# GroupNorm on one core: TensorE as a loop over the tiles, loads relayed into one count, and the last two tiles loaded in halves and stored in quarters

## The chip, the cores and the metric

The kernel runs on one core of one Trainium2 chip. The metric is the device time in microseconds (us) of that core. Most times below are medians of four or five runs, one of them profiled. The kernel before took 633.99 to 634.82 us, median 634.18, in the call that also timed the changed kernel.

## The reference

```python
# x: (128, 1024, 32, 16) bf16, g and b: (1024,) bf16, 32 groups of 32 channels
def reference(x, g, b):
    G = 32
    xr = x.reshape(B, G, C // G, H, W)
    mu = xr.mean(axis=(2, 3, 4), keepdims=True)
    var = ((xr - mu) ** 2).mean(axis=(2, 3, 4), keepdims=True)
    xn = ((xr - mu) / jnp.sqrt(var + 1e-5)).reshape(B, C, H, W)
    return xn * g[None, :, None, None] + b[None, :, None, None]
```

It reads 134.2 MB and writes as much. One tile is 4 samples times 32 groups on 128 partitions, with 16384 bf16 values (32 KB) in each: 4 MB. There are 32 tiles.

## The kernel before

SBUF holds a ring of six tile slots. SyncE issues all loads and stores. TensorE sums a tile with 32 matmuls against an identity matrix, VectorE turns the sum into the negative mean, ScalarE squares the tile around the mean in two passes of 7.12 us, and VectorE then scales and shifts in place, 32 operations a tile. Tile i+6 is loaded into the slot that tile i was stored from.

```python
SLOTS, RUN, MM_FREE = 6, 2, 512          # F = 16384 values a partition, NT = 32 tiles, NMM = 32

def on_sync(e):
    def load(j):
        if j >= SLOTS:
            e.wait_ge(st[j % SLOTS], 16 * (j // SLOTS))       # the slot's store has landed
        e.dma_start(out=slot(j), in_=x_v[j]).then_inc(ld[j % SLOTS], 16)
    for j in range(SLOTS):
        load(j)
    for i in range(NT):
        e.wait_ge(s_done, i + 1)
        e.dma_start(out=o_v[i], in_=slot(i)).then_inc(st[i % SLOTS] if i + SLOTS < NT else s_fin, 16)
        if i % RUN == RUN - 1:                                # two stores, then two loads
            first = i + 1 + SLOTS - RUN
            for j in range(first, min(first + RUN, NT)):
                load(j)
    e.wait_ge(s_fin, 16 * SLOTS)

def on_tensor(e):                                             # unrolled: 1024 matmuls in the program
    ...
    for i in range(NT):
        e.wait_ge(ld[i % SLOTS], 16 * (i // SLOTS + 1))
        if i >= 2:
            e.wait_ge(s_mean, i - 1)
        par = i % 2
        for k in range(NMM):
            last = e.matmul(out=ps[:, par * MM_FREE : (par + 1) * MM_FREE], lhsT=eye[:],
                            rhs=slot(i)[:, k * MM_FREE : (k + 1) * MM_FREE],
                            start=(k == 0), stop=(k == NMM - 1))
        last.then_inc(s_sum, 1)

def on_vector(e):                                             # a loop over the tiles, addresses from registers
    ...
    with nc.Fori(0, NT, 1, engines=[e.engine], head_slot={e.engine: 128}) as i:
        ...                                                   # mean, 1/std, scale, bias
        for k in range(KC):                                   # KC = 32
            a = ring[:, bass.ds((i % SLOTS) * F + k * HW, HW)]
            last = e.tensor_scalar(out=a, in0=a, scalar1=scl[:, k : k + 1], scalar2=bia[:, k : k + 1],
                                   op0=ALU.mult, op1=ALU.add)
        e.drain()
        e.sem_inc(s_done, 1)
```

## Time and profile before

| what | value |
| --- | --- |
| time | 634.18 us (633.99 to 634.82) |
| span of the profiled run | 632.4 us |
| DMA traffic | 268.4 MB, mean 425 GB/s |
| busy share | ACT 76%, DVE 60%, PE 42% |
| last data packet ends / last landing / span ends | 630.63 / 631.11 / 632.37 us |

These are lines of the profile's page of the kernel before: the span, the DMA and bandwidth rows of the span in 40 slices, the DMA queues with packets and MB, and the head of the chain that ended last.

```profile
span 632.4 us, 5262 instructions
...
DMA  8999999999999999999999999999999999999986
GB/s 365 430 430 421 435 431 430 431 431 431 431 426 431 433 435 433 432 435 427 433 431 426 435 433 429 430 427 433 433 433 434 435 435 435 431 430 431 431 386 276
...
q1 hardware_dynamic: 9216, 268.44, 98.8%
q8 instruction: 8, 0.13, 0.1%
...
DMA 69%; ACT 19%; PE 3%; DVE 2%; issue 2%; SPq 1%; DVEq 1%; ACTq 0%
```

The DMA row is at nine or more tenths from the second slice to the third last, and the bandwidth is level at about 431 GB/s. No engine is busy more than 76%. The sixteen DMA engines therefore bound the kernel. The bandwidth falls only in the last two slices, and that is what the change aims at. Queue 8 shows eight packets of instructions (16 KB each, 0.90 to 1.01 us): the unrolled TensorE program being fetched.

The chain of waits of the kernel before, its last part cut to the longest pieces (start, length, what), shows how it ends:

```profile
436.26 38.11 DMA out_dram<-ring
475.24 38.34 DMA out_dram<-ring
513.99 29.02 DMA out_dram<-ring
543.03 19.50 DMA ring<-in_x_dram
562.58 9.91 PE ps L135 x32
573.67 7.12 ACT ja L157
```

The chain runs through one store after the other and crosses to compute only at 562.6 us, for the last two tiles. A view of the last work on the engines of the kernel before (start, length, engine and line):

```profile
612.68 3.31 DVE L214 TENSOR_SCALAR ring<-ring,scl,bia  x10
616.05 0.33 SPq L103 DMA_DIRECT2D out_dram<-ring  x1
```

VectorE finishes at 615.99 us and the last store goes out at 616.05. This looks as if compute ended the kernel. The semaphore records say otherwise. Each transfer adds 16 to its semaphore, and the sixteen come apart. (That each is one DMA engine's is my reading: between 100 and 400 us 16.0 packets are under way on average, and a transfer is 128 packets of 32 KB, eight for each of sixteen.) The last store's first increment came at 626.96 us and its last at 631.11. The bandwidth rows of the DMA view from 600 to 640 us (40 slices of 1 us) of the kernel before show the hole that this leaves:

```profile
DMA  9999799999899663949999599930000000000000
GB/s 492 492 492 393 328 426 492 459 459 426 360 393 524 295 262 131 426 197 524 459 524 492 229 393 492 492 131 33 33 33 0 0 0 8 0 0 0 0 0 0
```

Between 613 and 616 us part of the engines have nothing to do (the row falls to six and three tenths), because the store isn't issued yet. From 627 us on only a few engines still move data, 33 GB/s, and from 628.6 us on one alone. That one had not been idle at all: it went from the store of tile 30 straight to that of tile 31.

### The profile page before, as it was taken

The page shows a single profiled execution, that of the slowest core. Times are in us where ns is not written, and L with a number is a line of the kernel's source. Part 1 is how long each engine was busy: PE and PEld are TensorE (multiplying, and loading weights), DVE is VectorE, ACT ScalarE, POOL GpSimd, SP SyncE. Part 2 cuts the span into 40 slices and gives each one's busy share as a digit, 9 for nine tenths or more (in the row PEclk, how much of TensorE's full clock was granted, in tenths as well). Part 3 has the DMA queues.
Part 4 walks back from the last instruction along what each step waited for, and adds up shares of the span by engine and source line. Part 5 has one row for each costly group of instructions (what it writes and reads, how often), then busy time and mean ns, then how long its engine had stood idle before and what let it go on. Part 6 is the DMA issues. An engine that isn't in the chain of part 4 may idle for free.

```text
span 632.4 us, 5262 instructions
## 1 busy us (share of the span) xinstructions
PE 265.1 (42%) x1025; PEld 107.4 (17%) x1025; DVE 378.0 (60%) x1189; ACT 481.1 (76%) x194; POOL 0.8 (0%) x6
## 2 busy tenths in 40 slices
PE   1987609064180641806327063270723608146000
PEld 0332203021030210302103021130301203012000
DVE  0047777777757277572765727567375672747770
ACT  0499999999979499593995949769597694967920
POOL 0000000000000000000000000000000000000000
PEclk9978759668595675956759577595875958759555
DMA  8999999999999999999999999999999999999986
GB/s 365 430 430 421 435 431 430 431 431 431 431 426 431 433 435 433 432 435 427 433 431 426 435 433 429 430 427 433 433 433 434 435 435 435 431 430 431 431 386 276
DMA packets 9321, 268.58 MB, mean 425 GB/s; under 512 B 1120, under 2 KB 1120, under 8 KB 1120
## 3 DMA queue, kind: packets, MB, share of 16 engines
q1 hardware_dynamic: 9216, 268.44, 98.8%
q8 instruction: 8, 0.13, 0.1%
q10 hardware_dynamic: 96, 0.00, 0.0%
q14 instruction: 1, 0.01, 0.0%
HBM read 134.22 MB, written 134.22 MB: 425 GB/s over the span
## 4 chain that ended last, share of the span: by engine, by line
DMA 69%; ACT 19%; PE 3%; DVE 2%; issue 2%; SPq 1%; DVEq 1%; ACTq 0%
DMA out_dram<-ring 64%; ACT ja L157 18%; DMA ring<-in_x_dram 5%; PE ps L135 3%; DVE ring L214 2%; DVEq L218 1%; SPq L103 1%; SPq L97 1%; ACT var L167 0%; DVEq L214 0%; ACTq L166 0%; ACTq L157 0%; ACT rstd L171 0%; DVE jd L185 0%; DVEq L200 0%
## 5 line engine op out<-in xcount | busy, mean ns | idle before, releaser
L157 ACT ACTIVATE ja<-ring,nm 128x8192 fp8e5 x64 | 455.8, 7122 | 116.8 <-DVE jd L185 111.4
L135 PE MATMUL ps<-ring,eye 128*128 128x512 bf16 x1024 | 264.9, 425 | 303.2 <-DMA ring<-in_x_dram 297.2
L214 DVE TENSOR_SCALAR ring<-ring,scl,bia x1024 | 333.6, 406 | 7.5 <-issue 7.5
L135 PEld LDWEIGHTS ps<-ring,eye 128*128 128x128 bf16 x1024 | 107.3, 107 | 460.5 <-DMA ring<-in_x_dram 311.2
L185 DVE TENSOR_SCALAR_CACHE_REDUCE jd<-ps 128x512 bf16 (+1 forms) x33 | 22.8, 691 | 153.0 <-PE ps L135 137.6
L201 DVE RECIPROCAL inv<-rstd 128x1 f32 x32 | 5.2, 164 | 59.1 <-ACT rstd L171 56.6
L157 ACT ACTIVATION_READ_ACCUMULATOR ja<-ring,nm 128x1 f32 x64 | 11.9, 186 | 0.0
L171 ACT ACTIVATE rstd<-sq,var 128x1 f32<-128x1 f32 x32 | 9.4, 294 | 2.2
L167 ACT ACTIVATE var<-sq,eps_t 128x1 f32<-128x1 f32 x32 | 9.4, 294 | 2.2
L207 DVE SCALAR_TENSOR_TENSOR bia<-scl,nm,gb 128x32 f32<-128x32 f32 x32 | 8.0, 251 | 4.7
L203 DVE TENSOR_SCALAR scl<-gb,inv 128x32 f32<-128x32 f32 x32 | 7.7, 241 | 2.5
L182 DVE COPY gb<-gb_p 128x64 f32<-128x64 f32 x1 | 0.2, 225 | 10.0 <-PE gb_p L128 10.0
L128 PE MATMUL gb_p<-gb_b,rep 32*128 32x64 bf16 x1 | 0.2, 205 | 11.0 <-DMA gb_b<-in_b_dram 11.0
L151 ACT ACT_TABLE_LOAD x1 | 1.3, 1283 | 1.9 <-issue 1.9
L185 DVE DVE_READ_ACCUMULATOR jd<-ps (+1 forms) x33 | 2.7, 83 | 0.0
L128 PEld LDWEIGHTS gb_p<-gb_b,rep 32*128 32x128 bf16 x1 | 0.1, 100 | 11.0 <-issue 11.0
L177 DVE MEMSET ones_b<- 128x128 bf16 x1 | 0.2, 165 | 1.1 <-SPq L221 1.1
L118 POOL TENSOR_SCALAR_AFFINE_SELECT rep<-ones_b 32x128 bf16<-32x128 bf16 x1 | 0.3, 302 | 0.0
L114 POOL TENSOR_SCALAR_AFFINE_SELECT eye<-ones_b 128x128 bf16<-128x128 bf16 x1 | 0.3, 292 | 0.9 <-DVEq L179 0.9
L151 ACT ACTIVATE warm<-eps_t 128x1 f32<-128x1 f32 x1 | 0.2, 203 | 0.0
L241 POOL MEMSET const-bfloat16-1.0<- 128x1 bf16 x1 | 0.1, 102 | 0.0
L241 POOL MEMSET const-uint8-127<- 128x1 uint8 x1 | 0.1, 102 | 0.0
(3 smaller groups left out, 0.3 us busy)
## 6 DMA issues: line engine op xcount, KB each, us to landing
ring<-in_x_dram SPq DMA_DIRECT2D x32, 4096.0 KB, 19.4
out_dram<-ring SPq DMA_DIRECT2D x32, 4096.0 KB, 29.2
gb_b<-in_g_dram ACTq DMA_DIRECT2D x1, 2.0 KB, 6.2
gb_b<-in_b_dram ACTq DMA_DIRECT2D x1, 2.0 KB, 9.5
```

Source lines behind the costliest of these rows:

```text
L97: e.dma_start(out=slot(j), in_=x_v[j]).then_inc(ld[j % SLOTS], 16)
L103: e.dma_start(out=o_v[i], in_=slot(i)).then_inc(st[i % SLOTS] if i + SLOTS < NT else s_fin, 16)
L135: last = e.matmul(out=ps[:, par * MM_FREE : (par + 1) * MM_FREE], lhsT=eye[:], rhs=slot(i)[:, k * MM_FREE : (k + 1) * MM_FREE], start=(k = ...
L157: e.activation(out=ja[:], in_=ring[:, bass.ds((i % SLOTS) * F + h * (F // 2), F // 2)], func=ACT.Square, bias=nm[:, par : par + 1], scale=1.0,
L167: e.activation(out=var[:], in_=sq[:, 0:1], func=ACT.Identity, bias=eps_t[:], scale=inv_n)
L171: e.activation(out=rstd[:, par : par + 1], in_=sq[:, 1:2], func=ACT.Sqrt, bias=var[:], scale=inv_n,).then_inc(s_rstd, 1)
L185: e.tensor_scalar(out=jd[:], in0=ps_i, scalar1=-inv_n, scalar2=None, op0=ALU.mult, op1=ALU.add, accum_out=nm_i,).then_inc(s_mean, 1)
L201: e.reciprocal(out=inv[:], in_=rstd[:, bass.ds(i % 2, 1)])
L203: e.tensor_scalar(out=scl[:], in0=gb[:, 0:KC], scalar1=inv[:], scalar2=None, op0=ALU.mult)
L207: e.scalar_tensor_tensor(out=bia[:], in0=scl[:], scalar=nm[:, bass.ds(i % 2, 1)], in1=gb[:, KC : 2 * KC], op0=ALU.mult, op1=ALU.add,)
L214: last = e.tensor_scalar(out=a, in0=a, scalar1=scl[:, k : k + 1], scalar2=bia[:, k : k + 1], op0=ALU.mult, op1=ALU.add,)
L218: e.drain()
```

## The change

The intent: take the eight instruction fetches away by making TensorE a loop; let GpSimd relay the six load semaphores into one count so that the loop can wait on a count; lay VectorE's whole program at a block's head instead of its loop alone; and let the last two tiles be loaded in halves and stored in quarters, so that compute starts and stores earlier. The diff, cut to its core:

```diff
+IN_PARTS = 2
+NH = 2
+NQ = 4
...
 # SyncE
-            e.dma_start(out=slot(j), in_=x_v[j]).then_inc(ld[j % SLOTS], 16)
+            for c in range(load_parts(j)):          # NH for the last two tiles, else 1
+                w = F // load_parts(j)
+                e.dma_start(out=slot(j)[:, c * w : (c + 1) * w], in_=x_v[j][:, c * w : (c + 1) * w]
+                ).then_inc(ld_of(j, c)[0], 16)
+        def store(i):
+            for c in range(store_parts(i)):         # NQ for the last two tiles, else 1
+                w = F // store_parts(i)
+                e.wait_ge(s_done, NQ * i + NQ // store_parts(i) * (c + 1))
+                e.dma_start(out=o_v[i][:, c * w : (c + 1) * w], in_=slot(i)[:, c * w : (c + 1) * w]
+                ).then_inc(st[i % SLOTS] if i + SLOTS < NT else s_fin, 16)
...
-        e.wait_ge(s_fin, 16 * SLOTS)
+        e.wait_ge(s_fin, 16 * sum(store_parts(i) for i in range(NT - SLOTS, NT)))
 # GpSimd
+        e.sem_inc(s_mean, 2)
...
+        for i in range(NT):
+            for c in range(load_parts(i)):
+                e.wait_ge(*ld_of(i, c))
+                e.sem_inc(s_ld, NH // load_parts(i))
 # TensorE
-        for i in range(NT):
-            e.wait_ge(ld[i % SLOTS], 16 * (i // SLOTS + 1))
-            if i >= 2:
-                e.wait_ge(s_mean, i - 1)
+        with nc.Fori(0, NT, 1, engines=[e.engine]) as i:
+            e.wait_ge(s_mean, i + 1)
             for k in range(NMM):
+                if k % (NMM // NH) == 0:
+                    e.wait_ge(s_ld, i * NH + k // (NMM // NH) + 1)
                 last = e.matmul(
-                    out=ps[:, par * MM_FREE : (par + 1) * MM_FREE],
+                    out=ps[:, bass.ds((i % 2) * MM_FREE, MM_FREE)],
                     lhsT=eye[:],
-                    rhs=slot(i)[:, k * MM_FREE : (k + 1) * MM_FREE],
+                    rhs=ring[:, bass.ds((i % SLOTS) * F + k * MM_FREE, MM_FREE)],
...
 # VectorE
+        e.addr_align(256, offset=128, max_nops=0)
...
-            e.drain()
-            e.sem_inc(s_done, 1)
+                if k % (KC // NQ) == KC // NQ - 1:  # after each quarter of the tile
+                    e.drain()
+                    e.sem_inc(s_done, 1)
```

In the loop the tile's place in the ring is not known when the program is built. Each matmul therefore gets an instruction before it that computes the address in a register. That is a side effect of `bass.ds((i % SLOTS) * F + ...)`.

More of the change, by code (lines that the diff above doesn't have):

```diff
@@ L83 @@
     ld = [sem(f"ld{s}") for s in range(SLOTS)]
+    ld_more = [sem(f"ldm{s}") for s in range(IN_PARTS * (NH - 1))]
     st = [sem(f"st{s}") for s in range(SLOTS)]
     s_gb, s_ones, s_eye, s_fin = sem("gbl"), sem("ones"), sem("eye"), sem("fin")
+    s_ld = sem("lds")
     s_gbp, s_sum, s_mean, s_rstd, s_done = (
@@ L88, with load_parts, ld_of, store_parts @@
     )
+    def load_parts(j):
+        return NH if j >= NT - IN_PARTS else 1
+    def ld_of(j, c):
+        if c == 0:
+            return ld[j % SLOTS], 16 * (j // SLOTS + 1)
+        return ld_more[(j - NT + IN_PARTS) * (NH - 1) + c - 1], 16
+    def store_parts(i):
+        return NQ if i >= NT - IN_PARTS else 1
     def slot(i):
@@ L96, in load @@
                 e.wait_ge(st[j % SLOTS], 16 * (j // SLOTS))
-            e.dma_start(out=slot(j), in_=x_v[j]).then_inc(ld[j % SLOTS], 16)
+            for c in range(load_parts(j)):
+                w = F // load_parts(j)
+                e.dma_start(
+                    out=slot(j)[:, c * w : (c + 1) * w], in_=x_v[j][:, c * w : (c + 1) * w]
+                ).then_inc(ld_of(j, c)[0], 16)
[3 more added lines that the diff above has]
+                e.wait_ge(s_done, NQ * i + NQ // store_parts(i) * (c + 1))
+                e.dma_start(
+                    out=o_v[i][:, c * w : (c + 1) * w], in_=slot(i)[:, c * w : (c + 1) * w]
+                ).then_inc(st[i % SLOTS] if i + SLOTS < NT else s_fin, 16)
         for j in range(SLOTS):
@@ L101, in on_sync @@
         for i in range(NT):
-            e.wait_ge(s_done, i + 1)
-            e.dma_start(out=o_v[i], in_=slot(i)).then_inc(
-                st[i % SLOTS] if i + SLOTS < NT else s_fin, 16
-            )
+            store(i)
             if i % RUN == RUN - 1:
@@ L128, in on_tensor @@
         e.matmul(out=gb_p[:], lhsT=rep[:], rhs=gb_b[:], start=True, stop=True).then_inc(s_gbp, 1)
-        for i in range(NT):
-            e.wait_ge(ld[i % SLOTS], 16 * (i // SLOTS + 1))
-            if i >= 2:
-                e.wait_ge(s_mean, i - 1)
-            par = i % 2
+        with nc.Fori(0, NT, 1, engines=[e.engine]) as i:
+            e.wait_ge(s_mean, i + 1)
             for k in range(NMM):
+                if k % (NMM // NH) == 0:
+                    e.wait_ge(s_ld, i * NH + k // (NMM // NH) + 1)
                 last = e.matmul(
-                    out=ps[:, par * MM_FREE : (par + 1) * MM_FREE],
+                    out=ps[:, bass.ds((i % 2) * MM_FREE, MM_FREE)],
                     lhsT=eye[:],
-                    rhs=slot(i)[:, k * MM_FREE : (k + 1) * MM_FREE],
+                    rhs=ring[:, bass.ds((i % SLOTS) * F + k * MM_FREE, MM_FREE)],
                     start=(k == 0),
@@ L142, in on_tensor @@
             last.then_inc(s_sum, 1)
-        e.wait_ge(s_mean, NT)
+        e.wait_ge(s_mean, NT + 2)
         e.sem_inc(s_sum, 1)
@@ L154, in on_scalar @@
                 i = i0 + par
-                e.wait_ge(s_mean, i + 1)
+                e.wait_ge(s_mean, i + 3)
                 for h in range(2):
@@ L192, in on_vector @@
         e.drain()
-        with nc.Fori(0, NT, 1, engines=[e.engine], head_slot={e.engine: 128}) as i:
+        with nc.Fori(0, NT, 1, engines=[e.engine]) as i:
             e.wait_ge(s_sum, i + 2)
@@ L213, in on_vector @@
                 a = ring[:, bass.ds((i % SLOTS) * F + k * HW, HW)]
-                last = e.tensor_scalar(
+                e.tensor_scalar(
                     out=a, in0=a, scalar1=scl[:, k : k + 1], scalar2=bia[:, k : k + 1],
```

## The prediction

> **What bounds the kernel now.** The DMA engines. The page's slices between the first and the last two stand at 421 to 435 GB/s, DMA share nine tenths or more. ACT is busy 76%, DVE 60%, PE 42%. The chain of waits is 64% stores; its ACT part (24 to 115 us) runs while the windows show a DMA share of 1.0, so the time doesn't hang on it. From 150 us on SP issues stores in pairs without waiting: compute is ahead.
>
> **Where time could be won.** The slices lose about 2.4 us at the head and 7.4 at the tail (365, 386 and 276 GB/s against 431). But the trace's packet and semaphore records say more. A 32 KB packet takes 1.213 us, and the 16 engines finish a transfer at different times: one semaphore's 16 increments spread over 0.5 us for the first load, 3.0 us at 62 us, 4.2 at 178, 5.6 at 381, 7.7 for the store of tile 30 (613.7 to 621.5 us). The last store is issued at 616.1; twelve engines then stood idle up to 3.3 us, but the slowest works on tile 30's store until 620.9, goes straight on and ends at 630.6. The span ends 1.7 us later. So the slowest engine, not VectorE's last tile, ends the kernel.[...]
>
> **What the change does, costed.**
> - TensorE's 1024 unrolled matmuls become 32 in a loop. The trace has eight 16 KB instruction packets (page, queue 8) about 78 us apart, each 0.9 to 1.0 us on one engine, whose next data packet is about 0.5 us late: 1.5 us to one engine each time. They vanish. Estimate from the increments: the slowest engine took one (at 39 us), so 0 to 2 us gained; the second slowest ends at 628.6, which caps a gain on the slowest alone at 2.0.
> - Each matmul gains an address instruction. VectorE's such pairs take 0.33 us; if TensorE's do, a tile takes 10.5 us instead of 7 to 10, with 19.4 available. Off the path.
> - GpSimd's relay: 0.2 us a load (estimate from semaphore hops of about 0.1). Off the path.
> - VectorE: three more drains[...]. Off the path; the block-head move costs nothing.
> - Halved loads: ScalarE starts tile 30 (573.7 us) 3 to 5 us earlier, since 16 matmuls instead of 32 remain after the landing.
> - Quartered stores: tile 31's first quarter goes out some 12 us earlier, the last about 4. This fills the twelve idle engines and moves the slowest by nothing. Smaller packets cost at most 0.5 us.
>
> **Prediction.** 632.7 us, range 631.0 to 634.5. Faster by over 2%: 1%; within 2%: 97%; slower: 2%.
>
> **What would show it right.** Instruction packets 8 to about 0; the dip to 197 GB/s at 614 to 616 us gone; VectorE's end 3 to 5 us earlier; yet the last data packet only 0 to 3 us earlier than 630.6, the last store's increments still spread over 4 us or more. TensorE at most 11 us a tile.
>
> **What would make it wrong.** If the engines' spread comes mostly from the fetches, the end comes 4 us or more earlier (below 630). If TensorE's loop fetches its code on every trip, or an address instruction costs over 0.5 us, TensorE comes on the path. If small packets cost more than their bytes, the tail grows.

The forecast came to 632.7 us, which is 634.2 less about 1.5. What is cut out of its text is a time for three more drains on VectorE, which no trace gave, and a reference; the drains stand as off the path, so no term of the 1.5 is cut. (The changed kernel's trace has VectorE idle for 0.21 us at each of them, about 0.65 us a tile.) The half microsecond that it has the data packet late after a fetch can be read off the kernel before: that packet takes 1.60 to 1.72 us, against the 1.213 of the others.

## The result, and the profile after

The changed kernel took 636.87 us (636.73 to 637.04, four runs). The ratio to the kernel before is 1.0041, 95% interval 1.0023 to 1.0058. A ratio here is the mean time of one kernel's runs over that of the other's of the same rounds, so it is not quite the ratio of the medians quoted. The change made the kernel slower by 2.7 us, and the predicted range ended at 634.5.

The same lines of the changed kernel's page:

```profile
span 635.3 us, 6588 instructions
...
DMA  8999999999999999999999999999999999999994
GB/s 362 429 437 421 429 431 427 435 433 435 435 429 429 429 429 437 431 439 435 429 429 429 429 435 431 431 429 427 423 433 421 437 427 419 427 427 431 429 416 205
...
q1 hardware_dynamic: 10368, 268.44, 98.7%
...
q14 instruction: 2, 0.02, 0.0%
...
DMA 51%; ACT 28%; PE 9%; DVEq 3%; DVE 3%; issue 2%; ACTq 1%; SPq 0%; POOLq 0%
...
L165 PE MATMUL ps<-ring,eye 128*128 x1024 | 254.6, 412 | 311.9 <-POOLq L154 300.2
```

The row of queue 8 is gone, so the fetches are gone. TensorE waits for GpSimd's relay where it waited for the loads, and for about as long (300.2 us against 297.2 us for the loads before), so the relay costs nothing visible. There are 1326 more instructions. The last but one slice rose from 386 to 416 GB/s, as intended, and the last fell from 276 to 205, because it lies later.

The last work on the engines of the changed kernel, and then its DMA view from 600 to 640 us:

```profile
612.73 1.05 DVE L245 TENSOR_SCALAR ring<-ring,scl,bia  x3
613.84 0.33 SPq L123 DMA_DIRECT2D out_dram<-ring  x1
```

```profile
DMA  9989998989999999999999999932110000000000
GB/s 492 459 360 393 426 459 344 418 369 459 401 426 410 451 418 426 393 467 418 426 410 467 401 426 418 434 148 90 66 49 25 25 33 0 0 8 0 0 0 0
```

The hole is filled, VectorE ends 2.2 us earlier (613.78 us), and the last store goes out 2.2 us earlier. Yet the last data packet ends at 633.29 us instead of 630.63. From about 626 us the bandwidth comes from few engines and in the end from one. The sixteen increments of the last store show it: the eight earliest come 0.2 to 0.5 us sooner than before, the eight others later, the last one by 2.6 us. So the tail did not lose the time. The tail is where it shows.

When did it arise? One view by stretches, for both kernels (the last two columns are DMA share and GB/s), first before, then after:

```profile
100.00:400.00 300.00, 124.53 (x493) 50.74 (x491) 195.24 (x614) 247.70 (x102) 0.00 (x0) 0.71 1.00 432
400.00:560.00 160.00, 65.50 (x256) 26.62 (x256) 97.89 (x309) 123.55 (x49) 0.00 (x0) 0.70 1.00 432
```

```profile
100.00:400.00 300.00, 121.87 (x490) 50.99 (x488) 197.59 (x608) 246.34 (x101) 0.00 (x0) 0.72 1.00 432
400.00:560.00 160.00, 63.86 (x256) 26.78 (x256) 99.06 (x305) 122.61 (x51) 0.00 (x0) 0.71 1.00 426
```

Up to 400 us the mean bandwidth is equal. From 400 to 560 us it is 426 against 432 GB/s. The mean hides the cause. I took each transfer's sixteen increments from the trace, sorted them, and set the last one, which is the slowest engine, against a steady pace of 9.685 us a transfer. This is how far the slowest engine stands behind that pace plus a constant, in us (the transfers are numbered by their end; the times are those of the first increment in the kernel before; the experiments' rows are explained below):

| kernel | 256 us | 372 us | 430 us | 488 us | 546 us |
| --- | --- | --- | --- | --- | --- |
| before | 18.26 | 18.94 | 18.93 | 19.19 | 20.16 |
| after | 18.16 | 19.41 | 20.53 | 21.12 | 22.37 |
| a3 (before with the split tail) | 17.80 | 18.71 | 18.71 | 19.07 | 20.03 |
| a4 (before with the loop) | 17.69 | 18.87 | 19.79 | 20.46 | 21.59 |
| e1 (loop, constant addresses) | 17.60 | 18.54 | 19.37 | 19.84 | 20.80 |
| e2 (address instructions, fetches kept) | 18.02 | 18.80 | 19.94 | 20.50 | 21.65 |
| e3 (no address instructions) | 18.88 | 19.61 | 19.59 | 19.57 | 19.55 |

The slowest engine of the changed kernel is level with that of the kernel before at 256 us and 2.2 us behind it at 546 us, which is most of the 2.7 us. (The median of the sixteen stands near 13.8 until about 300 us in both.) The two rows are not the same engine throughout. Until about 450 us the last engine of the kernel before is one that loses its time in a few steps (to 17.60 at 178 us, 18.26 at 256 and 18.93 at 333 us, each at a transfer that a fetch of 16 KB fell into) and stands still between them. Another one falls back steadily, starts at 14.52 at 120 us and is last only from 450 us on; that one sets the end. The trace doesn't name the engine of an increment, so the line of one engine is read off the sorted values. Read like that, one engine falls back 0.51 us in each round of four transfers (38.75 us) in the kernel before, and 0.70 us in the changed one, over the eleven rounds from 120 to 546 us. The loss comes in small amounts: a 32 KB packet takes 1.213 us, and in each round a few packets of that engine take 5 to 80 ns longer, mostly those of stores.

There is a second effect. From about 410 us on, the other engines of the changed kernel lose about 2 us too. A load is issued when the slowest engine has landed the store that it waits for: one landed at 427.17 us, its first increment 7.01 us earlier, and the load went out at 427.19. At 429.5 to 429.7 us three packets of 32 KB begin that take 1.6 to 2.5 us instead of 1.213; between 400 and 620 us the changed kernel has 58 packets over 1.3 us, the kernel before 12. I read this as the fast engines running out of queued work. They are ahead, so that ends nothing later.

### The profile page after: what moved, and what is told of

Read it like the earlier page. It is cut to its first block, busy times and chain, and to the rows that moved or that the text cites. A ratio compares the mean times of both kernels' runs of the same rounds, so it can differ in the third digit from the quotient of the medians.

```text
span 635.3 us, 6588 instructions
## 1 busy us (share of the span) xinstructions
PE 254.8 (40%) x1025; PEld 107.0 (17%) x1025; DVE 386.8 (61%) x1189; ACT 481.1 (76%) x194; POOL 0.8 (0%) x6
## 4 chain that ended last, share of the span: by engine, by line
DMA 51%; ACT 28%; PE 9%; DVEq 3%; DVE 3%; issue 2%; ACTq 1%; SPq 0%; POOLq 0%
DMA out_dram<-ring 34%; ACT ja L187 27%; DMA ring<-in_x_dram 17%; PE ps L165 9%; DVE ring L245 2%; DVEq L250 2%; DVEq L245 1%; ACT var L197 1%; DVEq L231 0%; ACTq L196 0%; ACT rstd L201 0%; ACTq L187 0%; DVE bia L238 0%; DVE scl L234 0%; DVE jd L216 0%
## 5 line engine op out<-in xcount | busy, mean ns | idle before, releaser
L165 PE MATMUL ps<-ring,eye 128*128 x1024 | 254.6, 412 | 311.9 <-POOLq L154 300.2
L245 DVE TENSOR_SCALAR ring<-ring,scl,bia x1024 | 342.3, 408 | 28.2 <-issue 28.2
## 6 DMA issues: line engine op xcount, KB each, us to landing
out_dram<-ring SPq DMA_DIRECT2D x30, 4096.0 KB, 29.2
```

The source lines that it names most:

```text
L165: last = e.matmul(out=ps[:, bass.ds((i % 2) * MM_FREE, MM_FREE)], lhsT=eye[:], rhs=ring[:, bass.ds((i % SLOTS) * F + k * MM_FREE, MM_FREE) ...
```

## The experiments

The expectations below carry labels. **T1**: the instruction fetches, each of which delays another engine, keep the sixteen engines out of step; without them the engines run in a bunch and take turns, and the disturbance falls on one. **T2** and **T3** put the loss on the other parts of the change: the split tail with its smaller packets, and the relay with the added drains and the moved program. **T4**: the loop costs by what its instructions do, whether there are fetches or not. **T6** is T4 in its last form: one DMA engine is delayed a little by each of the instructions that TensorE and VectorE execute, the address instructions above all. A label that isn't in this list is an intermediate form between T4 and T6; the conclusions don't need it.

The prediction was wrong and its cause was open after the first runs, so eighteen kernels were run. They were run at other times. Kernels are compared only within the same rounds. All gave correct results.

### The parts of the change, one at a time

**a1: the whole change without the split tail.**

```diff
 def load_parts(j):
-    return NH if j >= NT - IN_PARTS else 1
+    return 1
 def store_parts(i):
-    return NQ if i >= NT - IN_PARTS else 1
+    return 1
```

> The changed kernel with its last two tiles loaded and stored whole; all else as changed. Theory T1 (the unrolled TensorE program's instruction fetches delayed single DMA engines and so kept the 16 out of step; without them packets take longer from 400 us on): stays slow, 636 to 638 us. Theory T2 (the split tail costs it): back to 633 to 635. Theory T3 (VectorE's drains and block place change when stores are issued): stays slow, 636 to 638.

Measured: 636.25 us against 634.38 for the kernel before, ratio 1.0029 (1.0012 to 1.0045).

**a2: the whole change, but TensorE unrolled (relay, tail, drains and VectorE's place kept).**

```diff
-        with nc.Fori(0, NT, 1, engines=[e.engine]) as i:
+        for i in range(NT):
...
-                    rhs=ring[:, bass.ds((i % SLOTS) * F + k * MM_FREE, MM_FREE)],
+                    rhs=slot(i)[:, k * MM_FREE : (k + 1) * MM_FREE],
```

> The changed kernel with TensorE's matmuls unrolled again (relay, VectorE and tail as changed), so the eight instruction packets are back. T1: 633 to 635 us, and few packets over 1.3 us after 400 us. T2 and T3: 636 to 638.

Measured: 635.02 us, ratio 1.0008 (0.9992 to 1.0025).

**a3: the kernel before with the split tail and its drains only.** The edit is the SyncE and VectorE part of the diff above; the unrolled TensorE waits for the halves itself.

> The kernel before with the split tail and VectorE's four drains alone (TensorE unrolled, no relay, loop head where it was). T1: 632.5 to 634.5 us. T2: 636 to 638. T3 if it is the drains: 636 to 638.

Measured: 634.96 us, ratio 1.0010 (0.9993 to 1.0027).

**a4: the kernel before with the loop and the relay only.** The edit is the TensorE and GpSimd part of the diff above, without halves.

> The kernel before with TensorE's loop and GpSimd's relay alone (VectorE and tail as before). T1: 636 to 638 us, with long packets after 400 us. T2 and T3: 633 to 635.

Measured: 636.15 us, ratio 1.0029 (1.0012 to 1.0045). Its page:

```profile
span 633.9 us, 6450 instructions
...
q1 hardware_dynamic: 9216, 268.44, 98.7%
...
q14 instruction: 1, 0.01, 0.0%
```

What follows: in medians the loop costs 1.8 us (a4) and the tail 0.6 us (a3), and a2 with 0.6 us leaves at most 0.1 us for relay, drains and place. The loop alone has an interval clear of 1. The tail's interval spans 1, but a part of its cost is seen in every trace: from the last landing to the span's end it takes 1.26 us in the kernel before, a4 and a1, and 1.61 us in a3, a2 and the changed kernel. So the split stores cost 0.35 us after the last byte has landed. T2 and T3 fall as reasons of the main loss. The loop is the matter, and a4 differs from the kernel before in two things at once: no fetches, and about 1150 more instructions on TensorE, 1088 of them register instructions.

### Giving the loop its fetches back

**b1 and b2: a4 with 66, or 134, empty drains a tile on GpSimd, to make its program long enough to be fetched.**

```diff
             e.sem_inc(s_ld, 1)
+            for _ in range(66):      # b2: 134
+                e.drain()
```

> The kernel before with TensorE's loop and the relay, and 66 idle drains on GpSimd after each relayed load, so that GpSimd's program (not TensorE's) is fetched in 16 KB packets, 6 to 8 of them. T1 (the fetches keep the 16 engines out of step, and engines in step hurt the straggler at each turn from loads to stores): back from 636.2 to 634.0 to 635.3 us; the increments of a store in mid-run are spread evenly, not 13 or 14 within 1 us. T4 (the loop itself costs it, by its address instructions or its timing): stays 635.7 to 636.6.

> The same with 134 drains a tile: about 14 to 16 instruction packets. T1: 634 to 635.5 us, the spread even. A theory that fetches only delay (T5, my prediction's): each adds 1.5 us to one engine, so no gain over the loop without, 636 or more.

Measured: b1 638.15 us against 634.03, ratio 1.0061 (1.0044 to 1.0078); b2 647.51 us, ratio 1.0211 (1.0194 to 1.0228). T1 expected these to restore the time. They made it worse, and b1 lies above T4's range too. But the fetches weren't those of TensorE: they came as 17 more (b2: 34 more) packets of 8 KB on queue 14, 0.31 us each (16 KB was the size of TensorE's eight in the kernel before, and for GpSimd no trace had shown it), and fell on the same one or two engines, so the engines stayed bunched. T1 is neither shown nor refuted. What the increments show is that in b1 the last engine falls back in steps, one at each of these fetches, from 17.15 at 101 us to 20.40 at 295 us: 0.65 us a fetch, about twice the packet's own 0.31 us. The drains themselves are a rival for a part of the loss, since b1 executes 2112 more instructions; see the table of instructions below.

**b3 and b4: three stores and three loads in a run instead of two (RUN = 3), on the kernel before and on a4.**

```diff
-RUN = 2
+RUN = 3
```

> The kernel before with three loads and three stores in turn instead of two. T1: fewer turns, and one more transfer queued behind the awaited store, so the straggler loses less: 631.5 to 634 us. T4: no view; 634.4 unless the later loads leave the engines idle.

> TensorE's loop and relay with three in turn. T1: two thirds of the turns, so the loss of 1.8 us against the unrolled form with the same turns is 1.3 us or less, and the time is under that with two in turn (636.2). T4: 1.8 us above the unrolled form with three in turn.

Measured: b3 641.09 us (1.0103), b4 643.75 us (1.0154). RUN = 3 by itself loses time early: the engines stand idle for 1.3 us at about 82 us. The loop's cost on top of it is 2.7 us, not smaller than with RUN = 2. That speaks against the turns of T1, but the two kernels differ from the others in too much to decide.

### Half of the loop, and other ways to spread the engines

**c1: sixteen tiles unrolled, then a loop over sixteen. c2: the other way round.**

```diff
-        with nc.Fori(0, NT, 1, engines=[e.engine]) as i:
+        for i in range(0, 16):
+            ...                                      # unrolled, constant addresses
+        with nc.Fori(16, NT, 1, engines=[e.engine]) as i:
```

> The kernel before with the relay; TensorE's tiles 0 to 15 unrolled, 16 to 31 looped: about four instruction packets, all in the first half. T1 (engines once out of step stay so): 634 to 635.2 us, the engines still spread in the second half. T4 (the loop itself slows the straggler, and the loss falls after 330 us): as the full loop, 635.7 to 636.6.

> The other way round: tiles 0 to 15 looped, 16 to 31 unrolled, the packets in the second half. T1: the straggler has by then been alone for 300 us; between, 634.8 to 636. T4: 634 to 635, since the loss falls in the second half, where TensorE is unrolled again.

Measured, against 634.79: c1 635.34 us, ratio 1.0012 (0.9995 to 1.0028); c2 635.43 us, ratio 1.0010 (0.9993 to 1.0027). In medians either half of the loop costs about a third of the whole, but both intervals span 1, and neither time is where T4 had put it (635.7 or more, and 634 to 635; c2 lies in T1's range). The increments say more than the times. From 430 to 546 us, three rounds in which the steady engine can be told apart in every trace, it falls back 0.57 us a round in c1, which loops then, and 0.48 in c2, which is unrolled then. In the same stretch the unrolled kernels have 0.50 (before), 0.49 (a3) and 0.49 (a2), the looped ones 0.60 (a4), 0.61 (after) and 0.64 (a1). So the climb changes with the loop within one run, as T4 says. The fetches go with it, though: c2 has them in that stretch and c1 has none.

**c3: a4 with a 16 KB copy on GpSimd's queue every fourth tile. c4: a4 with five small copies at the start, meant to set the engines apart.**

```diff
+            if i % 4 == 1:                           # c3
+                e.dma_start(out=dump[n : n + 1, 0:8191], in_=x_d[n : n + 1, 0:8191]).then_inc(s_dump, 16)
...
+        for n, k in enumerate((2, 4, 6, 8, 10)):     # c4
+            e.dma_start(out=dump[16 * n : 16 * n + k, :], in_=x_d[16 * n : 16 * n + k, :]).then_inc(s_dump, 16)
```

> TensorE's loop and relay, with eight copies of one 16 KB row (HBM to an HBM scratch) issued by GpSimd, one every four tiles: delays like those of the fetches, but no instructions. T1: 634 to 635.5 us if the copies fall on different engines, and the engines spread. T4: 635.7 or more.

> TensorE's loop and relay, with five small copies after the first six loads that have 2, 4, 6, 8 and 10 rows of 16 KB[...]. T1: the straggler's loss after 60 us falls from 5 us to 3.5 or less; 634 to 635.5 us unless the straggler is one of the two engines put back most (then up to 637). T4: the loss stays 5 us; 636 or more.

Measured: c3 637.58 us (1.0044), c4 638.29 us (1.0058). Neither did to the engines what it was made for. In c3 the copies took 0.61 us each and the engines stayed in a bunch. In c4, as I read its trace, each copy was spread over all sixteen engines, so that none was set back alone.

**d1: a4 with sixteen small loads at the start, over 8 down to 1 partitions, meant to set back a part of the engines only.**

```diff
+        for n in range(16):
+            k = 8 - n // 2
+            e.dma_start(out=dump[8 * n : 8 * n + k, :], in_=x_v[0][8 * n : 8 * n + k, 0:2560]).then_inc(s_dump, 16)
```

> TensorE's loop and relay, with 16 small loads after the first six that have 8, 8, 7, 7, ... 1, 1 rows of 5 KB, so that up to eight engines start the first store 0.4 to 3 us behind. T1 (in step is what hurts): the slowest engine's loss from 62 us to the last store falls from 5 us towards before's 3.7, and the time to 634 to 635.5 us, unless the straggler is among the engines put back most (then the loss is to be read, not the time). Against T1: the engines stand spread over 3 us and the slowest still loses 5 us; 636 or more.

Measured, against 634.72: 638.22 us, ratio 1.0052 (1.0035 to 1.0069). Now the stagger worked. The trace doesn't name the engines, but eight of them stood 0.4 to 3.5 us behind the rest from 95 us on. The slowest engine climbed all the same, from 3.71 us to 7.24 us behind the first between 159 and 401 us and by 0.57 us a round from 430 to 546 us, near the 0.60 of a4. The engines were out of step and the climb stayed near the loop's. That speaks against T1; the time itself can't decide, since the stagger delays engines too. e1 below settles it.

**d2: the kernel before with its stores on ScalarE's queue (ScalarE unrolled for that). d3: d2 with a4's loop and relay.**

```diff
 # SyncE: loads only
+        for j in range(SLOTS, NT):
+            load(j)
 # ScalarE: after tile i's statistics
+            if i:
+                store(i - 1)
```

> The kernel before (TensorE unrolled) with stores issued by ScalarE on its own queue[...]. T1: no clusters of long packets at turns, the slowest engine falls behind less; 630 to 634.5 us. If mixed packets cost more than their bytes: slower than 634.4.

> The same with TensorE's loop and the relay. T1: without turns the loop costs nothing: within 0.6 us of the unrolled form. T4 (the loop itself): 1.8 us above it.

Measured: d2 636.67 us (635.87 to 639.6, ratio 1.0037, interval 1.0006 to 1.0068); d3 638.39 us (1.0055, 1.0038 to 1.0072). With two queues the order is another and costs 2 us by itself. In d2 a load takes 27.3 us from issue to landing instead of 19.4, and a store 43.6 instead of 29.2 (medians), which I take as loads and stores sharing the engines. The picture is clean: between 200 and 560 us only five packets of 32 KB take over 1.3 us in d2, each right after a fetch, and one in d3; the rest are small delays. The loop still costs 1.7 us in medians (d2's runs scatter by more than that, so the number is soft). The slowest engine of d3 stands at 22.64 at 145 us and at 27.36 at 551 us on the scale of the table above, 0.45 us a round; d2's slowest is level (22.86 to 23.37), and its climbing engine, read off the sorted values, needs 0.37 us a round from 430 to 546 us, against 0.44 in d3. In d2 and d3 no engine ends behind the rest: the increments of the last store come within 0.16 us of each other. With hardly a long packet left the climb is there all the same (0.44 us a round in d3), so it needs no clusters of long packets at turns.

### Instructions against fetches

What was left: the loop's address instructions, or the missing fetches by some way other than T1. These two were separated with the same number of matmuls and of bytes.

**e1: TensorE loops over six tiles a trip.** In each trip tile c lies in slot c, so every address is a constant, and the wait can go to the slot's own semaphore; no relay.

```diff
+        with nc.Fori(0, NT // SLOTS, 1, engines=[e.engine]) as trip:
+            for c in range(SLOTS):
+                i = trip * SLOTS + c
+                e.wait_ge(ld[c], 16 * (trip + 1))
+                e.wait_ge(s_mean, i + 1)
+                for k in range(NMM):
+                    last = e.matmul(out=ps[:, (c % 2) * MM_FREE : (c % 2 + 1) * MM_FREE], lhsT=eye[:],
+                                    rhs=slot(c)[:, k * MM_FREE : (k + 1) * MM_FREE], ...)
+        ...                                          # the last two tiles, the same way
```

> The kernel before with TensorE's loop over six tiles a trip, so that every address is a constant: no fetches in the run, no address instructions, no relay. T6 (the address instructions slow one DMA engine's packets a little each): the drag of small delays is that of before, about 0.54 us a round, and the time 632.5 to 634.6 us. T1 (the missing fetches leave the engines in step): as the full loop, 635.6 to 636.6.

Measured, against 634.36 (five rounds): 634.69 us, ratio 1.0006 (0.9993 to 1.0020). Its page:

```profile
span 633.3 us, 5281 instructions
...
q8 instruction: 2, 0.03, 0.0%
```

A loop, two fetches instead of eight, and no loss clear of noise. T1 expected 635.6 to 636.6 here; its engines run in a bunch, and yet the climb is 0.48 us a round from 430 to 546 us, as unrolled. T1 falls. (T6's range ended at 634.6, 0.1 us lower.) The missing fetches and the loop as such cost nothing measurable. They gain nothing either.

**e2: two trips of sixteen unrolled tiles, with the ring address computed as in the changed kernel.**

```diff
+        with nc.Fori(0, 2, 1, engines=[e.engine]) as half:
+            for c in range(NT // 2):
+                i = half * (NT // 2) + c
+                ...
+                        rhs=ring[:, bass.ds((i % SLOTS) * F + k * MM_FREE, MM_FREE)],
```

> TensorE's loop with two trips of 16 tiles each and the relay: address instructions before every matmul as in the full loop, but 16 tiles' code unrolled, so that it is fetched in the course of the run. T6: drag 0.6 us a round or more, 635.5 to 637 us. T1: as before, 634 to 635.

Measured: 635.54 us, ratio 1.0018 (1.0004 to 1.0031). Its page:

```profile
span 633.9 us, 6358 instructions
...
q8 instruction: 6, 0.10, 0.1%
```

Six fetches (between 31 and 265 us) are back, and so are 1026 address instructions, and 1.2 us are lost. All five runs (635.09 us or more) lie above all five of e1 (635.0 or less). From 430 to 546 us, where no fetch falls in either, e2's engine falls back 0.57 us a round and e1's 0.48. The loss goes with the instructions, not with the fetches. At 546 us its slowest engine is where a4's is (21.65 and 21.59 in the table).

**e3: e1, and VectorE too loops over six tiles a trip with constant addresses.** This takes away the address instructions that the kernel before had all along.

```diff
-            a = ring[:, bass.ds((i % SLOTS) * F + k * HW, HW)]
+            a = slot(c)[:, k * HW : (k + 1) * HW]
...
+        with nc.Fori(0, NT // SLOTS, 1, engines=[e.engine], head_slot={e.engine: 0}) as trip:
+            for c in range(SLOTS):
+                tile(trip * SLOTS + c, c)
+        ...                                          # the last two tiles, the same way
```

> e1 with VectorE's loop over six tiles a trip too, so that its 1024 address instructions go as well. T6: the drag falls clearly under before's, to 0.4 us a round or less, and the time to 631 to 633.8 us, under before. T1, or if only TensorE's instructions count: as e1, within 0.4 us.

Measured: 633.08 us (632.72 to 633.15, five runs), ratio 0.9980 (0.9967 to 0.9994). Its page, and its stretches:

```profile
span 631.0 us, 4046 instructions
...
GB/s 366 431 429 411 437 434 432 433 432 434 434 432 432 428 434 432 432 432 430 432 432 428 432 432 432 432 432 434 436 432 434 430 434 434 432 429 434 432 422 260
...
q8 instruction: 2, 0.03, 0.0%
```

```profile
100.00:400.00 300.00, 124.43 (x498) 50.82 (x496) 194.72 (x612) 246.19 (x97) 0.00 (x0) 0.72 1.00 433
400.00:560.00 160.00, 65.38 (x256) 26.59 (x256) 98.28 (x310) 123.79 (x51) 0.00 (x0) 0.69 1.00 432
```

It is the fastest kernel, faster than both the kernel before and the changed one, by a little: its slowest run (633.15) is below the fastest of the kernel before in that call (633.89). The climbing engine falls back 0.41 us a round instead of e1's 0.54, and it no longer ends last: at 546 us it stands at 19.06, and the engine at 19.55, which had lost most of its time by 139 us (18.25), stands still from 372 us on. Between 400 and 560 us the bandwidth is 432 GB/s, where the changed kernel has 426, and in the slices it stays level up to the last but one (422).

All kernels with whole tiles that keep the transfers of the kernel before and add nothing else, with the page's count of instructions, the time against the kernel before of the same call, and the climb of the steady engine, over eleven rounds from 120 us where I read it and over the last three from 430 us:

| kernel | instructions | us against before | us a round | from 430 us |
| --- | --- | --- | --- | --- |
| e3 | 4046 | -1.28 | 0.41 | 0.38 |
| before | 5262 | 0 | 0.51 | 0.50 |
| e1 | 5281 | +0.33 | 0.54 | 0.48 |
| c1, c2 | 5874 | +0.55, +0.64 | | 0.57, 0.48 |
| e2 | 6358 | +1.18 | | 0.57 |
| a4 | 6450 | +1.77 | 0.62 | 0.60 |
| a1 | 6578 | +1.87 | 0.63 | 0.64 |

A straight line through these (fitted by least squares) rises 1.2 us for 1000 instructions and misses none by more than 0.3 us. The kernels with the split tail lie above it, by 0.4 us or 1.0: a3 (5346, +0.58), a2 (5383, +0.64), and the changed kernel (6588, +2.69). The line is a summary and no law: b1 (8562, +4.12) happens to lie on it, b2 (10738, +13.48) is 6.9 us above it. Nor need every instruction count alike. b1's drains on GpSimd did not raise the small delays between 62 and 295 us (0.50 us a round, summed over all engines' packets that take 2 to 100 ns over 1.213 us, against 0.54 in a4 and 0.51 in the kernel before).

## Why the prediction was wrong, point by point

- **"The DMA engines" bound it, and "the slowest engine, not VectorE's last tile, ends the kernel": right.** The changed kernel's last work was issued 2.2 us earlier and landed 2.6 us later. (The last store's increments spread over 4.15 us before and 7.27 us after, by the first and last of the sixteen.)
- **The split tail "fills the twelve idle engines and moves the slowest by nothing": right.** The hole at 614 to 616 us is gone, ScalarE starts tile 30 at 570.53 instead of 573.67 us (3.1 us earlier, 3 to 5 predicted), and a3 gained nothing. VectorE ended 2.2 us earlier; 3 to 5 had been predicted.
- **"Instruction packets 8 to about 0": right. "0 to 2 us gained" from it: nothing was gained.** e1 has two fetches instead of eight and takes 634.69 us against 634.36, with an interval of the ratio that holds 1. The size was the wrong end of the range. As far as the sorted values show, the fetches of the kernel before delayed, from 120 us on, other engines than the one that is last from 450 us on.
- **"Each matmul gains an address instruction ... Off the path": this is the step that failed.** It was costed as TensorE's time only, and there it was right: a tile takes TensorE 7.1 to 9.5 us, at most 11 predicted. But the instructions cost elsewhere. With about 1100 of them more, the slowest DMA engine, which is never idle and has no slack, falls back 0.62 us a round instead of 0.51, and the kernel ends 1.8 us later (a4). Constant addresses in the same kind of loop lose nothing (e1), the addresses without the short loop lose (e2), and taking VectorE's away as well gains (e3).
- **"Smaller packets cost at most 0.5 us": too small.** The tail measured 0.6 us in medians (a3, a2), of which 0.35 us lie after the last landing: 1.61 us to the end of the span against 1.26. The wait for the last store is not where they go: SyncE goes on 0.02 us after the last landing with six stores on that count and with twelve. They lie between its next drain and the semaphore instruction after it (0.08 us before, 0.43 in the changed kernel); why is not shown. For the packets alone 0.5 us would have done: in the changed kernel 32 KB take 1.213 us, 16 KB 0.611 and 8 KB 0.309 (medians). As an estimate from these three, an engine's 16 load packets in halves and 16 store packets in quarters take 0.5 us longer.
- **Relay and drains "off the path", the block-head move "costs nothing": right,** at most 0.1 us in all (a2 against a3). With the relay and the loop the first matmul of a tile starts 0.38 us after the load's landing instead of 0.05 (medians of the changed kernel and the kernel before); 0.2 had been estimated for the relay.

In sum: predicted 632.7, which is 634.2 less about 1.5. Measured: 634.18 + 1.77 (address instructions) + 0.58 (tail) = 636.53, against 636.87; the rest of 0.3 us is within the scatter of the runs.

What stays open. It is shown that the time goes with the address instructions of TensorE, and that the loss appears as small delays of one DMA engine's packets. For VectorE's, e3 fits, but its gain has a possible second reason, since its VectorE program differs in its pace as well. No run parts the address instruction from the matmul that takes its address from a register, so either may do it. How it delays a DMA engine isn't shown, nor why it is this one engine. Nor was it tested whether the loss is one of measuring: timed and profiled runs of a kernel agree within their scatter, but every run gives a span and a clock, so none is known to have run unobserved. The order of the kernels under the metric is not touched by this.

## What to carry to other kernels

When DMA engines bound a kernel, read the sixteen increments of the transfers and not only the mean bandwidth: here the engine that was last decided, and work that filled the others gained nothing (a3: 634.96 us against 634.38). That its own engine had slack did not make an instruction free here. If a loop must be made, run it over as many tiles as the ring has slots, so that the addresses are constants (e3: 633.08 us against 634.36, e1: 634.69, where computed addresses gave 636.15 against 634.38 in a4). Test the parts of a change apart before explaining their sum, for here one part was expected to gain and lost, and a plausible mechanism (T1) stood until e1 refuted it.
